# Attention heads among two weight-heavy layers: moving each reader of TensorE's results one slot behind it, and third-block scores to the front

## The chip, the cores and the metric

The kernel runs on one core of one Trainium2 chip. The metric is the device time of one execution in microseconds (us). TensorE (PE) multiplies matrices into PSUM; VectorE (DVE), ScalarE (ACT) and GpSimd (POOL) do the elementwise work; SyncE (SP) issues the DMAs. Each engine works through its own instructions in the order in which the program gives them.

## What is computed

Windowed causal attention with a linear position bias, then two dense layers with activations, all in float32:

```python
scores = scale * np.matmul(q, k.transpose(0, 1, 3, 2))     # 4 batches, 8 heads, 576 x 576, head size 64
scores = np.where(mask, scores + bias[None], -1e9)         # mask: 0 <= row - column < 128
attn = np.exp(scores - scores.max(-1, keepdims=True))
attn = attn / (attn.sum(-1, keepdims=True) + 1e-9)
x = np.matmul(attn, v)                                     # 2304 tokens x 512 (heads side by side)
h = x @ w_in                                               # 512 -> 2048
x = (h * np.clip(h + 3, 0, 6) / 6) @ w_out                 # 2048 -> 512
g = s * np.maximum(x @ w_in2, 0) ** 2 + b
out = g @ w_out2
```

## The kernel before

**Slots.** Everything up to the second layer is laid out by hand: `at(slot, rank, fn)` puts a step into a numbered slot, and the program is written slot by slot, by rank within one. Loads have rank 0 to 1, the matmuls of the first layer 10, attention matmuls 20 and more, elementwise work 30 and more. Nothing reorders it later, so an instruction that must wait holds up everything behind it on its own engine.

**The first layer** works on eight groups of tokens (four batches, first rows 0 to 255, then rows 256 to 575), each in 16 `Step`s. A step's `h` (L605) is twelve matmuls into one PSUM bank of its own tag, which all groups but the last share; `relu` (ACT, L616), `product` (DVE, L619), `hi` (ACT, L626) and `lo` (DVE, L630) turn it into two parts, and `o` (L643, twelve matmuls) of the step is four slots behind `h`. For groups 2 to 6 an odd slot holds o and h, an even slot only attention matmuls; relu and product are in the slot after h, hi and lo in the one after that. For groups 0 and 1, whose steps alternate, and for the last group h lies in the even slot.

**The heads.** Groups 0 and 1 take their heads from `StartUnit` (not changed). Those of groups 2 to 7, two at a time, are `Unit`s, planned 20 slots and more ahead of their group's first step; pairs start at slots 29, 37, 45 and so on. In what follows a place is a slot counted from a pair's first one, modulo 8. A pair goes through `load` and `load_values` (DMA), `scale` (ACT, L321), `scores` (PE, L339), `minima` (DVE, L352 and L353), `exps` (ACT, L363), `sums` (DVE, L370 and L373), `weights` (POOL, L379), `transposes` (PE, L388), `fold` (ACT, L392), `lower` (DVE, L401), `masks` (POOL, L413), `values` (PE, L428), `to_hi` (ACT, L439) and `to_lo` (DVE, L443). Groups 2 and 3 have two blocks of 128 rows a head; groups 4 to 7 have a third one of 64 rows, whose scores go into a second PSUM tile. Fold and lower read the same PSUM tile, fold first. The F tile that fold writes has one buffer.

**Places before the change.** First scores at 3, third scores at 7; minima of the even head at 3 and of the odd one at 5, of third blocks at 7 and 0; sums at 1 and 2, weights at 2 and 3; transposes, fold and lower of the even head at 4, of the odd one at 6; masks at 5 and 7; values at 1; to_hi at 2, to_lo at 3.

**PSUM.** `bank` (L148) hands out tiles. From slot 23 on three banks serve all scores, transposes and values, and the conversions of the first layer's weights. A tile asked for when none is free waits for one to be given up.

**Beside it** run the preparations of weights: `Half` (first layer, up to slot 65; L207 to L231) and `Pair` (second layer; from slot 76, every ten slots from 113 on; ACT L734, L737, L792, DVE L741, L746, L777, L796, POOL L752 and L796). Their DVE operations have ranks 37 and 38, behind those of the step and in part of the heads.

Of the kernel before, what the change touches and what calls it, by code (L numbers as in the profile page):

```python
# [23 lines left out]
def tile_alibi_window_attention_moe_moe2(  # L24
# [52 lines left out]
    def at(slot, rank, fn):  # L77
        plan.setdefault(slot, []).append((rank, len(plan[slot]), fn))
# [69 lines left out]
    def bank(name):  # L148

        nonlocal nbank  # L150
        free = 4 if slot < FIRST else 2 if slot < hslot[1, 0] else 0
        nbank += 1
        k = nbank % (3 + free)
        if k < free:
            return ps_o.tile([P, 512], F32, tag=f"o{3 - k}", name=name)
        return ps_w.tile([P, 512], F32, tag="a", bufs=3, name=name)
# [18 lines left out]
    class Half:  # L175
# [5 lines left out]
        def __init__(self, f, i, stage):  # L181
            self.f, self.i, self.stage = f, i, stage
            self.id = f"{f}_{i}"
            self.c = slice(i * DM, (i + 1) * DM)

        def plan(self, s):
            at(s - 3, 1, self.load)
            at(s, 30.1, self.high)
            at(s, 38, self.sign)
            at(s + 1, 31, self.add)  # L190
            at(s + 2, 31.2, self.hi)
            at(s + 3, 31, self.lo)

        def load(self):
            if self.stage is None:
                raw = raw_half()
            else:
                raw = wtile(self.stage, [P, 4 * DM], I32, f"stage{self.id}")[:, : 2 * DM]
            src = w1[self.f].bitcast(I32)
            nc.sync.dma_start(out=raw, in_=src[:, 2 * self.i * DM : 2 * (self.i + 1) * DM])  # L200
            raw = raw.rearrange("p (c w) -> p c w", w=2)
            self.l, self.h = raw[:, :, 0], raw[:, :, 1]
# [54 lines left out]
    class Unit:  # L257


        def __init__(self, g, b, qa, qb, h):  # L260
            self.g, self.b, self.qa, self.qb, self.h = g, b, qa, qb, h
            self.ka = max(0, qa - 1)
            self.nq = min(qb * P, S) - qa * P
            self.nk = min(qb * P, S) - self.ka * P
            self.nkb = qb - self.ka
            self.id = f"{b}_{qa}_{h}"

        def plan(self, s):
            two = min(self.qa + 2, self.qb)
            odd = self.h % 2  # L270
            s -= 4 * odd
            if not odd:
                at(s - 7, 1, self.load)
                at(s + 1, 1, self.load_values)
                at(s - 1, 34, self.scale)
                at(s + 3, 20, lambda: self.scores(self.qa, two))
                at(s + 7, 20, lambda: self.scores(two, self.qb))
            at(s + 3 + 2 * odd, 32, lambda: self.minima(self.qa, two))
            at(s + 7 + odd, 32.7, lambda: self.minima(two, self.qb))
            at(s + 5 + odd, 33, lambda: self.exps(self.qa, two))  # L280
            at(s + 8 + odd, 33, lambda: self.exps(two, self.qb))
            at(s + 9 + odd, 32.2, self.sums)
            at(s + 10 + odd, 33, self.weights)
            at(s + 12 + 2 * odd, 20, self.transposes)
            at(s + 12 + 2 * odd, 35, self.fold)
            at(s + 12 + 2 * odd, 35, self.lower)
            at(s + 13 + 2 * odd, 30.02, self.masks)
            if odd:
                at(s + 17, 20, self.values)
                at(s + 18, 39, self.to_hi)  # L290
                at(s + 19, 39, self.to_lo)

        def pair(self):
            return units[self.g * H + self.h // 2 * 2 :][:2]
# [1 line left out]
        def load(self):  # L296
            i, b = (1, self.b) if self.qa else (0, self.b - NATIVE)
            n = (self.qb - self.qa) * P
            raw = ap.tile([P, 832], F32, tag="raw", name=f"raw{self.id}")[:, : n + self.nk]
            if self.nq < n:  # L300
                nc.gpsimd.memset(raw[:, self.nq : n], 0.0)
            for u in self.pair():
                u.p = slice((u.h % 2) * D, (u.h % 2 + 1) * D)
                src = qk[i][b, u.h, u.p]
                nc.sync.dma_start(out=raw[u.p, n:], in_=src[:, self.nq :])
                nc.sync.dma_start(out=raw[u.p, : self.nq], in_=src[:, : self.nq])
                u.q = raw[:, : self.nq]
                u.X = raw[u.p, :n]
                u.rk = raw[u.p, n:]

        def load_values(self):
            i, b = (1, self.b) if self.qa else (0, self.b - NATIVE)
            rv = ap.tile([P, 2, 4 * D], F32, tag="v", bufs=2, name=f"rv{self.id}")
            rv = rv[:, :, : self.nkb * D]
            nc.sync.dma_start(out=rv, in_=vv[i][b, self.h // 2])
            for u in self.pair():
                u.rv = rv[:, u.h % 2].rearrange("p (n d) -> p n d", d=D)
# [5 lines left out]
        def square(self, i):  # L323
            o = (i - self.qa) % 2 * 256
            k0 = max(0, i - 1) * P
            k1 = min((i + 1) * P, S)
            return self.ps[(i - self.qa) // 2][:, o : o + k1 - k0], k0, k1

        def scores(self, a, b):
            for u in self.pair():  # L330
                if a == self.qa:
                    u.ps = []
                if a < b:
                    u.ps.append(bank(f"s{u.id}_{a}"))
            for i in range(a, b):
                for u in self.pair():
                    sl, k0, k1 = u.square(i)
                    q = (i - self.qa) * P
                    nc.tensor.matmul(  # L339
                        sl, lhsT=u.X[:, q : q + P], rhs=u.rk[:, k0 - self.ka * P : k1 - self.ka * P],  # L340
                        start=True, stop=True,
                    )

        def minima(self, a, b):
            if a == self.qa:
                self.Pt = ap.tile([P, 3, P], F32, tag="P", bufs=5, name=f"P{self.id}")
                self.st = ap.tile([P, 3, 3], F32, tag="st", bufs=6, name=f"st{self.id}")
            for i in range(a, b):
                sl = self.square(i)[0]
                li, r = i - self.qa, rows(i)  # L350
                if i:
                    nc.vector.copy_predicated(out=sl[:, :r], mask=own[:, :r], data=sl[:, P:])  # L352
                nc.vector.tensor_tensor_reduce(  # L353
                    out=self.Pt[:, li], in0=sl[:, :P], in1=rel if i else rel0,
                    scale=slopes[self.h], scalar=3.0e38, op0=ALU.add, op1=ALU.min,
                    accum_out=self.st[:, 0, li : li + 1],
                )
# [745 lines left out]
    for f in range(NF):  # L1103
        for i, s in enumerate((hslot[0, f], oslot[0, f])):
# [3 lines left out]
            s = min(s - 6, 3 + 4 * f + 2 * i)  # L1108
# [19 lines left out]
    for t in range(nt2):  # L1128
        u = Tokens(t)
# [118 lines left out]
```

## Time and profile before

| what | value |
|---|---|
| median of the runs shown (3) | 952.02 us (951.62 to 953.02) |
| the profiled execution | 950.19 us |
| its span, first to last instruction | 948.5 us |
| mean granted clock of TensorE in it | 0.994 |
| PE busy in the span | 904.2 us, 95% |
| DVE, ACT, POOL busy | 689.2, 508.5, 427.1 us (73, 54, 45%) |

The times in the rows below are those of the profiled execution, counted from the start of its span. A row of the timeline gives the start, the time until its last instruction ended, the engine, the line of the program, the operation, what it writes and reads, and how many instructions are merged in the row; behind it, in brackets, how long the engine had been idle and what ended that. In a row of waits stand the waiting engine and line, what it waited for, the sum in us, how many times, and the longest. Matmuls overlap, so a step's length on PE is best read from the start of its first matmul to the start of the next step's.

### The profile page before, as it was taken

To read this page: it belongs to the slowest core of one execution; us is meant where nothing else is said; L and a number is where in the kernel's file an instruction comes from. 1 tells how busy PE (TensorE), PEld (TensorE's weight loads), DVE (VectorE), ACT (ScalarE), POOL (GpSimd) and SP (SyncE) were. 2 spreads that over 40 slices of the span, in tenths; PEclk is the share of its full clock that TensorE was granted. 3 is DMA by queue.
4 is the path that set the end of the run, shared out by engine and by line. 5 is a ranking of instruction groups with operands and counts; after the bars stand their busy time and mean duration, and the time that the engine had idled before them with its cause. 6 is when DMAs were issued, how large, how long until landed. Compare 5 with 4: busy or idle time off the path is not lost.

```text
span 948.5 us, 17831 instructions
## 1 busy us (share of the span) xinstructions
PE 904.2 (95%) x6514; PEld 847.6 (89%) x6517; DVE 689.2 (73%) x1489; ACT 508.5 (54%) x1211; POOL 427.1 (45%) x563
## 2 busy tenths in 40 slices
PE   8899789899999999999999999999899997999998
PEld 4598789889898889898989999998899996999998
DVE  7999885665777766677665746779837799377792
ACT  6988665455656555555544434563415644155441
POOL 6623331323454453445442312469334497233862
PEclk9999999999999999999999999999999999999999
DMA  9443333517365446444537446874779773787763
GB/s 332 143 158 101 106 101 91 177 29 235 116 219 177 151 150 205 151 159 158 173 123 254 153 166 218 303 271 168 259 267 328 261 254 146 248 297 248 271 237 115
DMA packets 62919, 183.08 MB, mean 193 GB/s; under 512 B 7152, under 2 KB 26736, under 8 KB 54384
## 3 DMA queue, kind: packets, MB, share of 16 engines
q1 hardware_dynamic: 62832, 181.95, 56.0%
q8 instruction: 51, 0.84, 0.4%
q14 instruction: 36, 0.29, 0.1%
HBM read 143.13 MB, written 38.80 MB: 192 GB/s over the span
## 4 chain that ended last, share of the span: by engine, by line
PE 76%; DVE 15%; ACT 4%; issue 3%; DMA 1%; POOL 0%; DVEq 0%; ACTq 0%; POOLq 0%
PE h L605 19%; PE h L1045 18%; PE o L643 16%; PE o L966 15%; PE s L339 3%; DVE i L949 3%; PE v L428 3%; DVE z L212 1%; DVE x L882 1%; PE t L388 1%; DVE t L619 1%; DVE raw L746 1%; DMA wstream<-wo 1%; ACT z L207 1%; ACT F L392 1%
## 5 line engine op out<-in xcount | busy, mean ns | idle before, releaser
L605 PE MATMUL h<-x,w 128*128 128x256 f32 (+1 forms) x1536 | 230.8, 299 | 20.5 <-DVE t L619 19.9
L605 PEld LDWEIGHTS h<-x,w 128*128 128x128 f32 x1536 | 211.4, 190 | 27.6 <-DVE t L619 26.0
L643 PE MATMUL o<-g,w 128*128 128x256 f32 (+1 forms) x1536 | 235.2, 302 | 0.8 <-DVE g L630 0.6
L643 PEld LDWEIGHTS o<-g,w 128*128 128x128 f32 x1536 | 209.8, 189 | 16.5 <-issue 9.0
L966 PE MATMUL o<-wstream,i 128*128 128x256 f32 x1512 | 186.9, 286 | 13.0 <-DVE i L949 12.7
L966 PEld LDWEIGHTS o<-wstream,i 128*128 128x128 f32 x1512 | 185.2, 195 | 14.6 <-DVE i L949 14.6
L1045 PE MATMUL h<-x,wstream 128*128 128x384 f32 x1008 | 175.4, 334 | 0.0
L1045 PEld LDWEIGHTS h<-x,wstream 128*128 128x128 f32 x1008 | 174.7, 188 | 0.0
L413 POOL TENSOR_SCALAR_AFFINE_SELECT W<-F 128x128 f32<-128x128 f32 (+1 forms) x144 | 46.0, 352 | 129.6 <-ACT F L392 127.6
L619 DVE SCALAR_TENSOR_TENSOR t<-t,h 128x256 f32<-128x256 f32 (+1 forms) x128 | 57.5, 449 | 62.2 <-ACT t L616 61.7
L949 DVE TENSOR_TENSOR i<-g,i 128x768 fp32r<-128x768 f32 x60 | 95.7, 1651 | 6.2 <-issue 5.0
L616 ACT ACTIVATE t<-h 128x256 f32<-128x256 f32 (+1 forms) x128 | 52.2, 408 | 88.3 <-PE h L605 88.2
L960 POOL TENSOR_TENSOR g<-g 128x768 f32<-128x768 f32 x36 | 86.5, 2428 | 0.0
L630 DVE TENSOR_TENSOR g<-t,g 128x256 fp32r<-128x256 f32 (+1 forms) x128 | 70.6, 551 | 14.6 <-ACT g L626 13.6
L379 POOL TENSOR_SCALAR P<-P,st 128x128 f32<-128x128 f32 x128 | 54.9, 444 | 44.6 <-DVE st L373 43.9
L626 ACT ACTIVATE g<-t 128x256 fp32r<-128x256 f32 (+1 forms) x128 | 56.5, 441 | 33.8 <-DVE t L619 33.2
L1082 ACT ACTIVATE g<-g,b_sb,s_sb 128x384 f32<-128x384 f32 x96 | 62.6, 699 | 3.3 <-DVE g L1069 3.3
L401 DVE TENSOR_TENSOR W<-t,tri 128x256 f32<-128x256 f32 x48 | 20.4, 424 | 55.8 <-ACT F L392 55.5
L392 ACT ACTIVATE F<-t 128x320 f32<-128x320 f32 (+1 forms) x48 | 20.0, 417 | 70.6 <-PE t L388 70.6
L1069 DVE SCALAR_TENSOR_TENSOR g<-g 128x384 f32<-128x384 f32 x72 | 55.5, 770 | 2.5
L1090 POOL TENSOR_TENSOR i<-g,i 128x384 fp32r<-128x384 f32 x24 | 24.7, 1031 | 66.7 <-ACT i L1086 66.7
L363 ACT ACTIVATE P<-P,st 128x128 f32<-128x128 f32 x128 | 50.3, 397 | 4.0 <-DVE st L353 3.4
(119 smaller groups left out, 1213.0 us busy)
## 6 DMA issues: line engine op xcount, KB each, us to landing
wstream<-wo SPq DMA_DIRECT2D x42, 1024.0 KB, 4.9
raw<-w SPq DMA_DIRECT2D x53, 512.0 KB, 5.1
wstream<-wh SPq DMA_DIRECT2D x24, 1024.0 KB, 5.3
wstream<-wh SPq DMA_DIRECT2D x24, 768.0 KB, 4.7
wh<-staging_early SPq DMA_DIRECT2D x16, 512.0 KB, 3.2
wo<-staging_early SPq DMA_DIRECT2D x12, 512.0 KB, 3.4
stage<-w SPq DMA_DIRECT2D x11, 512.0 KB, 4.8
out<-u SPq DMA_DIRECT2D x11, 384.0 KB, 3.3
```

Source lines behind the costliest of these rows:

```text
L379: nc.gpsimd.tensor_scalar(out=pt, in0=pt, scalar1=self.st[:, 2, li : li + 1], scalar2=1.0, op0=ALU.mult, op1=ALU.mult,)
L605: nc.tensor.matmul(self.ps, lhsT=w[:, wp, cc * P : (cc + 1) * P], rhs=x[:, cc, xp], start=m == 0, stop=m == 3 * CC - 1,)
L619: nc.vector.scalar_tensor_tensor(out=self.a, in0=self.a, scalar=6.0, in1=self.ps, op0=ALU.min, op1=ALU.mult)
L626: nc.scalar.activation(self.g[:, 0], self.a, AF.Copy)
L630: nc.vector.tensor_tensor(out=self.g[:, 1], in0=self.a, in1=hi, op=ALU.subtract)
L643: nc.tensor.matmul(acc[t][d], lhsT=w[:, wp, DM + d * P : DM + (d + 1) * P], rhs=self.g[:, gp], start=f == 0 and i == 0 and (t > 1 or d % 2 ...
L949: nc.vector.tensor_tensor(out=out[:, :, 1], in0=src, in1=out[:, :, 0].bitcast(F32), op=ALU.subtract)
L960: nc.gpsimd.tensor_tensor(out=out, in0=a, in1=b, op=op)
L966: nc.tensor.matmul(self.acc[k][c], lhsT=g[:, gp, c * P : (c + 1) * P], rhs=w[:, wp * HB : (wp + 1) * HB], start=p == 0 and i == 0, stop=p ...
L1045: nc.tensor.matmul(ps, lhsT=w[:, wp, cc], rhs=x[:, cc, xp], start=start and m == 0, stop=m == 5, skip_group_check=True,)
L1069: nc.vector.scalar_tensor_tensor(out=g, in0=g, scalar=0.0, in1=g, op0=ALU.max, op1=ALU.mult)
L1082: nc.scalar.activation(g, g, AF.Identity, scale=s_sb, bias=b_sb)
```

## The change

Only `Unit` is changed. Scores of third blocks go to place 1 (rank 20.5, behind the values of an earlier pair), their minima for both heads to 2 and exponentials to 3. First scores stay at place 3, at rank 20.5. Their minima go to 4 (even) and 5 (odd), exponentials stay at 5 and 6. Sums go to 6 and 7, weights to 7 and 0 (three slots earlier within a pair). Transposes go to 3 and 5, in front of the scores of place 3. Fold and lower stay at 4 and 6 with ranks 30.3 and 32.1 in place of 35. to_hi stays at 2 with rank 30.4 in place of 39; to_lo goes to 2. `scale` stays in its slot with rank 30.5 in place of 34. Since third blocks now come first, the bookkeeping of the two score tiles and of the P tile changes with them.

```diff
+            self.Pt = None
...
-                at(s - 1, 34, self.scale)
-                at(s + 3, 20, lambda: self.scores(self.qa, two))
-                at(s + 7, 20, lambda: self.scores(two, self.qb))
-            at(s + 3 + 2 * odd, 32, lambda: self.minima(self.qa, two))
-            at(s + 7 + odd, 32.7, lambda: self.minima(two, self.qb))
+                at(s - 1, 30.5, self.scale)
+                at(s + 1, 20.5, lambda: self.scores(two, self.qb))
+                at(s + 3, 20.5, lambda: self.scores(self.qa, two))
+            at(s + 2, 32, lambda: self.minima(two, self.qb))
+            at(s + 3, 33, lambda: self.exps(two, self.qb))
+            at(s + 4 + odd, 32, lambda: self.minima(self.qa, two))
             at(s + 5 + odd, 33, lambda: self.exps(self.qa, two))
-            at(s + 8 + odd, 33, lambda: self.exps(two, self.qb))
-            at(s + 9 + odd, 32.2, self.sums)
-            at(s + 10 + odd, 33, self.weights)
-            at(s + 12 + 2 * odd, 20, self.transposes)
-            at(s + 12 + 2 * odd, 35, self.fold)
-            at(s + 12 + 2 * odd, 35, self.lower)
-            at(s + 13 + 2 * odd, 30.02, self.masks)
+            at(s + 6 + odd, 32.2, self.sums)
+            at(s + 7 + odd, 33, self.weights)
+            k = s + 2 * odd
+            at(k + 11, 20, self.transposes)
+            at(k + 12, 30.3, self.fold)
+            at(k + 12, 32.1, self.lower)
+            at(k + 13, 30.02, self.masks)
             if odd:
                 at(s + 17, 20, self.values)
-                at(s + 18, 39, self.to_hi)
-                at(s + 19, 39, self.to_lo)
+                at(s + 18, 30.4, self.to_hi)
+                at(s + 18, 39, self.to_lo)
...
-            return self.ps[(i - self.qa) // 2][:, o : o + k1 - k0], k0, k1
+            return self.ps[-1 if i < self.qa + 2 else 0][:, o : o + k1 - k0], k0, k1
...
-            if a == self.qa:
+            if self.Pt is None:
                 self.Pt = ap.tile([P, 3, P], F32, tag="P", bufs=5, name=f"P{self.id}")
```

## Rows read from the trace of the kernel before

**Rows 1.** The page's part 1: busy time, share of the span, instructions.

```profile
PE 904.2 (95%) x6514; PEld 847.6 (89%) x6517; DVE 689.2 (73%) x1489; ACT 508.5 (54%) x1211; POOL 427.1 (45%) x563
```

**Rows 2.** Waits of PE from 75 to 140 us: sum, times, longest.

```profile
PE h L605 <- DVE t L619: 8.0, 4, 2.5
PE s L339 <- DVE raw L215: 1.1, 1, 1.1
```

**Rows 3.** Waits of PE from 140 to 260 us.

```profile
PE h L605 <- DVE t L619: 5.2, 6, 2.2
```

**Rows 4.** Waits of PE from 260 to 505 us.

```profile
PE h L605 <- DVE t L619: 6.0, 11, 0.9
```

**Rows 5.** Waits of all engines from 75 to 505 us.

```profile
ACT F L392 <- PE t L388: 70.6, 40, 3.6
...
DVE W L401 <- ACT F L392: 55.5, 41, 2.4
```

**Rows 6.** Timeline of all engines around one pause of PE, 300 to 305 us.

```profile
300.03 0.48 DVE L630 TENSOR_TENSOR g<-t,g 128x320 fp32r<-128x320 f32 x1
...
301.35 0.49 PE L388 MATMUL t<-ident,P 128*128 128x128 f32 x3
...
301.59 2.00 PE L643 MATMUL o<-g,w 128*128 128x320 f32 x12
301.87 0.44 ACT L392 ACTIVATE F<-t 128x320 f32<-128x320 f32 x1 [3.15 <-PE t L388]
...
302.34 0.42 DVE L401 TENSOR_TENSOR W<-t,tri 128x256 f32<-128x256 f32 x1 [1.83 <-ACT F L392]
...
302.68 1.31 DVE L746 SCALAR_TENSOR_TENSOR raw<-raw,work 128x1024 int32<-128x1024 int32 x1
...
303.92 0.47 DVE L619 SCALAR_TENSOR_TENSOR t<-t,h 128x320 f32<-128x320 f32 x1
...
304.45 2.04 PE L605 MATMUL h<-x,w 128*128 128x320 f32 x12 [0.85 <-DVE t L619]
```

**Rows 7.** PE's part of the same timeline over the turn that follows.

```profile
306.33 0.49 PE L388 MATMUL t<-ident,P 128*128 128x128 f32 x3
...
306.75 0.60 PE L339 MATMUL s<-raw 64*128 64x192 f32 x4
...
312.37 2.02 PE L643 MATMUL o<-g,w 128*128 128x320 f32 x12
...
314.23 1.92 PE L605 MATMUL h<-x,w 128*128 128x320 f32 x12
...
316.08 1.13 PE L339 MATMUL s<-raw 64*128 64x256 f32 x8
...
319.01 1.93 PE L605 MATMUL h<-x,w 128*128 128x320 f32 x12
...
320.77 0.49 PE L388 MATMUL t<-ident,P 128*128 128x128 f32 x3
```

**Rows 8.** Timeline in one of the long pauses before 140 us, DVE.

```profile
131.04 0.42 DVE L401 TENSOR_TENSOR W<-t,tri 128x256 f32<-128x256 f32 x1 [1.42 <-ACT F L392]
```

**Rows 9.** Timelines of POOL and of DVE, 165 to 168 us.

```profile
165.42 1.89 POOL L752 TENSOR_TENSOR raw<-raw 128x1024 int32<-128x1024 int32 x1 [5.62 <-ACT y L656]
...
166.10 1.49 DVE L630 TENSOR_TENSOR g<-t,g 128x256 fp32r<-128x256 f32 x1
```

**Rows 10.** DVE's part of the timeline of rows 7.

```profile
314.30 0.49 DVE L630 TENSOR_TENSOR g<-t,g 128x320 fp32r<-128x320 f32 x1 [0.76 <-ACT g L626]
...
315.00 0.67 DVE L796 TENSOR_TENSOR raw<-work,raw 128x512 fp32r<-128x512 f32 x1
...
317.25 0.30 DVE L352 COPY_PREDICATED s<-own,s 128x128 f32<-128x128 int32 x1
...
318.46 0.49 DVE L443 TENSOR_TENSOR x<-v,x 128x320 fp32r<-128x320 f32 x1
```

**Rows 11.** Busy time of the engines and PE's granted clock, 115.4 to 118.6 us.

```profile
115.40:118.60 3.20, 3.20 (x17) 2.27 (x17) 2.65 (x8) 2.39 (x6) 0.00 (x0) 0.50 0.00 0
```

More of the change, by code (lines that the diff above doesn't have):

```diff
@@ L309, in load @@
                 u.rk = raw[u.p, n:]
+                u.ps = []
         def load_values(self):
@@ L326, in square @@
             k1 = min((i + 1) * P, S)
-            return self.ps[(i - self.qa) // 2][:, o : o + k1 - k0], k0, k1
+            return self.ps[-1 if i < self.qa + 2 else 0][:, o : o + k1 - k0], k0, k1
         def scores(self, a, b):
             for u in self.pair():
-                if a == self.qa:
-                    u.ps = []
-                if a < b:
-                    u.ps.append(bank(f"s{u.id}_{a}"))
+                u.ps.append(bank(f"s{u.id}_{a}")) if a < b else None
             for i in range(a, b):
@@ L344, in minima @@
         def minima(self, a, b):
-            if a == self.qa:
+            if self.Pt is None:
                 self.Pt = ap.tile([P, 3, P], F32, tag="P", bufs=5, name=f"P{self.id}")
```

## The prediction

> **What bounds the kernel now.** I read the busy shares first: TensorE (PE) is busy 95% of the span [rows 1], more than VectorE (DVE), ScalarE (ACT) or GpSimd (POOL). So time is won only where PE stands still or does work that can go. Next I read who keeps PE waiting in the stretch where the later heads run, 75 to 505 us. Nearly all of it is one wait: the h-matmuls of a step (L605) wait for the product of the step before (DVE, L619), because all h-sums of groups 0 to 6 share one PSUM bank. It is 8.0 us in 4 waits up to 140 us, 5.2 us in 6 up to 260 us, and 6.0 us in 11 after that [rows 2 to 4]. The reader should see 21 pauses, not a steady loss.
>
> Then I read what DVE itself waits for: 55.5 us, 41 times, `lower` (L401) waits for `fold` (ACT, L392), which reads the same bank before it; and fold waits 70.6 us, 40 times, for the transposes [rows 5]. One pause shows how the two hang together [rows 6]. PE does h, then the transposes at 301.35, then o at 301.59. Fold and lower stand in the slot of the transposes, so ACT sits idle 3.15 us until PE has made them, and DVE idles 1.83 us before lower at 302.34. Queued behind lower are a long operation of the weight preparation (L746, 1.31 us) and the product, which starts at 303.92. PE, done with o, waits for it until 304.45. DVE was not short of time; it waited and then had to do everything at once. From o's first matmul to the next h 2.86 us pass here, against 1.86 where nothing waits (312.37 to 314.23) [rows 6, 7]: the pause costs 1.00 us and is recorded as 0.85 idle, so I add 0.15 us to every recorded wait.
>
> **The change part by part.** I count places 0 to 7 in the eight-slot turn of a pair, its first slot being 0; for the middle groups o and h come at even places.
>
> Fold, lower and transposes: transposes go to places 3 and 5, fold and lower stay at 4 and 6, ahead of the Pair operations. PE now runs a whole o and h between the transposes and the product that follows, so neither fold nor lower waits for PE. After 260 us the waits are 6.0 + 11 x 0.15 = 7.6 us [rows 4], and DVE's 1.83 us of idleness in the typical pause exceeds its 1.00 us of loss [rows 6]. I take all 7.6; bounds 3 and 7.6, since minima is added to place 4. Between 140 and 260 us they are 5.2 + 6 x 0.15 = 6.1 [rows 3]; the longest (2.2) lies where Pair 0 crowds several operations into one slot and stays in part, so I take 4.0; bounds 2 and 6.1.
>
> Up to 140 us the weights of the first layer are still being prepared (Half). There fold waits for no transpose: it stands behind exponentials and conversions on ACT, DVE idles 1.42 us in front of lower at 131.04 [rows 8], and the product comes later still. The ACT burst is not moved; fold only passes the exponentials of its slot. Of 8.0 + 4 x 0.15 = 8.6 us [rows 2] I take 1.0 as gained; bounds 0 and 8.6.
>
> Scores: third-block scores move from place 7 (behind the odd transposes) to 1 (behind the values), and the even transposes from o-and-h's place 4 to 3, ahead of the other scores. PE's runs of attention work in a turn go from four (values; scores; transposes; transposes with third scores) to three. A run costs PE at its edges: o after one takes 1.86, h before scores 1.85 (314.23 to 316.08), against 1.76 before a transpose (319.01 to 320.77) [rows 7]: 0.09 and 0.10. Changing from transposes to scores inside a run takes 0.42 (306.33 to 306.75) where transposes to o take 0.24 (301.35 to 301.59) [rows 6, 7], so 0.18. Before, a turn pays 2 x 0.19 for values and for scores, some 0.08 and 0.28 for the transposes; after, 0.19, 0.28 and 0.08, plus 0 to 0.2 for changing from values to scores, which no row shows. The saving is 0 to 0.19 in 16 turns (groups 4 to 7, four pairs each): 1.5, bounds 0 and 3. The eight turns of groups 2 and 3 have no third block and I put them at nothing.
>
> Minima, exponentials, sums, weights: the instructions are the same in number. Two full blocks of minima take 1.21 us of DVE (317.25 to 318.46) [rows 10], and the two narrower third blocks at place 2 no more. Even minima go from place 3 to 4, in front of lower, and odd ones stay at 5. Sums go from places 1 and 2 to 6 and 7, so that one head's stand in front of the product behind place 6: two operations on three columns, between nothing and one block of minima (0.6); I take 0.4. All of it lies under PE's 3.6 us of o and h unless a Pair operation of 1.3 us or more falls into places 5 and 6; that happens about once in five turns, and I charge 0 to 0.8 us each time, 1.0 in all.
>
> To_lo and the banks: `to_lo` (L443) goes from the end of place 3 to the end of place 2, because place 3 now takes all three free banks (even transposes, two scores). The last score must wait until to_lo has given up the values' bank. What is queued in front of to_lo on DVE? By the old trace, lo at 314.30, then the thirds' minima (up to 1.2, new), then L796 at 0.67 (315.00, now later), then to_lo at 0.49: done near 317.0. The last score would start near 317.15 (316.08, half a microsecond later for the third scores moved ahead, 0.57 for transposes and first score) [rows 7, 10]. That just fits; with L746 in L796's place (1.31) it is 0.5 late. I charge 2.0 us over the run; bounds 0 and the rival below.
>
> The rest: `scale` and `to_hi` only pass other ACT work in their slots; their pair's load is still issued eight slots before the first score, so at SP's queue I see no price. Fold has one F tile, which the masks on POOL read in the next slot: the odd fold, two slots on, waits only if POOL is over 3 us behind. Weights leave places 2 and 3 for 7 and 0, three slots or more ahead of the transposes. If those covers were gone, a late fold would hold relu and then the product as now. I put them at nothing; the bounds above hold them.
>
> **Sum:** 7.6 + 4.0 + 1.0 + 1.5 - 1.0 - 2.0 = 11.1 us. The profiled execution took 950.19 us (span 948.5), 1.83 below the median of the runs, 952.02. Against the profile it gives 939.1, against the median 940.9.
>
> **A rule that speaks against it.** At 166.10 lo (L630), 0.48 us at 300.03 [rows 9, 6], took 1.49 us, while POOL's L752 ran from 165.42 for 1.89 us: DVE's subtraction ended shortly after POOL was through [rows 9]. The Trainium skill ("SBUF — State Buffer", SBUF: two separate sides) says that DVE operations with two SBUF inputs and GpSimd operations share a port pair as an exclusive lock, and the loser waits for the whole instruction. The trace agrees. By that rule the moved POOL work decides anew which subtractions lose, and the sum comes out as in rival 1, or unchanged if no more of them lose than now.
>
> **Rivals.**
> 1. *POOL takes the gain back.* Weights and masks now meet other DVE subtractions; one collision costs 1.0 us [rows 9, 6]. For: lo, the Pair subtractions and POOL's long operations share the same slots. Against: POOL is busy only 45% [rows 1]. With half a microsecond uncovered in half of the 24 turns, 6 us go back: 947.
> 2. *The banks stop PE: slower.* Place 3 needs three banks, and to_lo is last in DVE's slot. For: the trace has one such wait, scores for L215, 1.1 us [rows 2]; to_lo now runs 2.4 us after the scores begin (316.08 to 318.46) [rows 7, 10]. Against: product and minima, which are in front of it now, then stand behind it. At 1.1 us in each of 24 turns it costs 26 us against a gain without it of 14.1 - 1.0 = 13.1 (the 1.0 being the crowding): 965. The point of balance is 13.1/24 = 0.55 us a turn.
> 3. *The early stage is freed too.* If fold's earlier rank and the lighter places 1 and 2 take away most of the 8.6 us [rows 2] too, and with them the stretch from 115.4 to 118.6 us in which the granted clock was 0.50, that is 1.2 GHz, just behind such a pause [rows 11], another 6 to 9 us go: 934. Against: ACT is full there [rows 8].
> 4. *It does nothing:* the product is as late by minima and sums in front of it as it was by lower. Then 952. Against: DVE's idle time in rows 5.
>
> **How the numbers follow.** My forecast (8 to 15 us gained) gets 0.57, rival 1 (2 to 8 gained) 0.17, rival 3 0.12, rival 4 0.05, rival 2 0.09. The likeliest gives 941. The range takes in the bounds of the forecast's costs, all of rival 1 and most of rival 3, down to 932 and up to 949; rivals 2 and 4 and the rest of 3 are left out. Measurements of this kernel can tell about 0.2%, 1.9 us. Faster by more: 0.57 + 0.17 + 0.12 = 0.86; same 0.05; slower 0.09.
>
> **What would show it.** Right: L401 and L392 no longer wait (55.5 us near zero), L605's wait for L619 after 140 us falls from 11.2 to under 4, PE shows values and third scores as one run. Wrong: scores or transposes waiting for L443 by several microseconds (rival 2), L619 still late behind L353, L373 or a stretched L630 (rivals 1 and 4). A wait for PE at fold or lower of its old size would make the whole prediction wrong.

## The result and the profile after

The changed kernel takes 943.49 us in the median of five runs (941.91 to 947.97), against 952.24 us (951.62 to 953.02) for the kernel before in the same runs: a ratio of 0.9917, 95% interval 0.9888 to 0.9947. That is 8.75 us less by the medians. The profiled execution took 942.24 us; its span is 940.5 us against 948.5, so 8.0 us less.

The page's part 1, kernel after:

```profile
PE 901.5 (96%) x6514; PEld 848.0 (90%) x6517; DVE 692.2 (74%) x1489; ACT 505.0 (54%) x1211; POOL 437.1 (46%) x563
```

As in [rows 1], PE is the only engine near its limit, and every engine has as many instructions as before. By stretches, as in [rows 2 to 4], the waits of PE are (after; 75 to 140, 140 to 260 and 260 to 505 us in this order):

```profile
PE h L605 <- DVE t L619: 8.1, 4, 2.1
PE s L339 <- DVE stage L215: 0.7, 1, 0.7
...
PE h L605 <- DVE t L619: 2.2, 2, 1.4
...
PE s L339 <- DVE x L443: 1.2, 2, 0.8
PE o L643 <- DVE g L630: 0.8, 1, 0.8
PE h L605 <- DVE t L619: 0.4, 2, 0.2
```

Up to 140 us nothing moved (8.0 to 8.1). After that L605's wait for L619 fell from 11.2 us in 17 waits to 2.6 in 4, and new waits appeared: scores for `to_lo` (L443) and o for `lo` (L630). The waits of all engines from 75 to 505 us, as in [rows 5]:

```profile
DVE t L619 <- ACT t L616: 69.5, 66, 2.6
DVE g L630 <- ACT g L626: 23.5, 41, 1.7
...
DVE W L401 <- ACT F L392: 3.2, 6, 0.7
```

`lower` waiting for `fold` is down from 55.5 us, 41 times, to 3.2 us, 6 times; fold's wait for the transposes (70.6 us) has left the list. The two long waits of DVE that remain are those of the steps themselves: the product waits for `relu` (69.5 us), `lo` for `hi` (23.5 us).

**Reading the gain by steps.** Both kernels run the same h and o on PE in the same order (only attention matmuls move among them), so the start of a step in one timeline less its start in the other is the lead won so far. I take three marks: the 27th h on PE (141.20 us before), the 58th (261.81) and the first matmul of the second layer, L1045 (569.34 before, 561.37 after). The last two columns are the lead won between the first mark and the third, and how many stretches of 3.4 us at a granted clock of 0.50 (1.2 GHz) the profile has between 75 and 145 us. The kernels of the experiments stand in the same table:

```
lead over before, us   27th h   58th h   layer 2   end of span   won 27th h to layer 2   at 1.2 GHz, 75-145
before                   0.0      0.0      0.0        0.0               0.0                  1
after                    1.69     4.39     7.97       8.0               6.28                 0
after_again             -1.16     1.55     5.15       3.7               6.31                 2
readers_alone           -2.82     0.49     6.66       6.7               9.48                 2
sums_behind              0.36     4.75     9.64       6.7               9.28                 3
sums_again               0.66     5.07     9.97       8.7               9.31                 2
tolo_ahead              -1.53     1.19     5.97       4.5               7.50                 2
sign_behind              0.67     3.42     7.01       5.5               6.34                 0
all_behind               2.38     4.88     9.39       6.4               7.01                 0
early_pool              -3.84     0.55     5.47       5.4               9.31                 3
before_sign             -5.09    -5.08    -4.99      -5.0               0.10                 2
minima_at_4             -1.74    -2.64    -2.56      -2.5              -0.82                 2
fold_back               -3.17    -7.22   -13.66     -16.6             -10.49                 3
fold_back_sums          -1.42    -3.28    -8.78     -10.3              -7.36                 1
```

The reader should see two things. Between the first and the third mark the clock is full in these profiles (fold_back and minima_at_4 have one stretch each there), and the two executions of the changed program agree to 0.03 us (6.28 and 6.31): this is what the change does. At the first mark they differ by 2.85 us, with no slow stretch in the one and two in the other. Two rows of busy time by window, after first, then its repetition (columns: time, then busy us and instructions of PE, PEld, DVE, ACT, POOL, granted clock, DMA share, GB/s):

```profile
75.00:140.00 65.00, 55.60 (x442) 50.81 (x441) 58.20 (x144) 47.49 (x122) 28.67 (x38) 1.00 0.35 109
```

```profile
75.00:140.00 65.00, 56.38 (x425) 51.36 (x423) 57.43 (x137) 46.28 (x120) 28.32 (x37) 0.95 0.36 108
```

The kernel before had 0.97 in this window, with the one stretch of [rows 11]. So the 1.69 us by which after leads at the 27th h are no shorter waits (8.0 and 8.1 us). At 75 us the lead was 0.27; it fell to -2.00 at the 15th h and was back at -0.12 at the 21st; then 1.49 us came between the 21st and the 22nd h, where only the kernel before has a stretch at half the clock.

**Where the lead after 140 us comes from.** The lengths of three pieces in ten successive turns (from about 294 us on), each from its first matmul to the next piece's first: o at place 6, o at place 0, and the two blocks of scores at place 3.

```
before          o at 6: 2.85 1.84 2.32 1.84 2.52 2.86 1.84 2.32 1.84 2.52
                o at 0: 1.90 2.23 1.86 1.86 1.86 1.90 2.23 1.86 1.86 1.86
                scores: 1.06 in all ten
after           o at 6: 1.84 1.84 1.84 1.84 1.83 1.84 1.84 1.84 1.84 1.84
                o at 0: 1.76 2.17 1.76 1.76 2.42 1.76 1.88 1.76 1.76 2.42
                scores: 1.37 1.06 1.06 1.06 2.50 1.06 1.06 1.06 2.16 1.06
```

All the old pauses are gone, at both places. New ones stand at place 0 and in the scores, fewer but not smaller. The 2.17 in the second turn at place 0 is one of them, not the old 2.23: lower waits for nothing there, but lower, the sums and a Pair operation (L746) are queued in front of the product. Where nothing waits, o at place 0 takes 1.76 in place of 1.86, since no attention matmuls stand before it any more.

### The profile page after: what moved, and what is told of

The parts are those of the page before. It is cut to its first block, busy times and chain, and to the rows that moved or that the text cites. A ratio compares the mean times of both kernels' runs of the same rounds, so it can differ in the third digit from the quotient of the medians.

```text
span 940.5 us, 17984 instructions
## 1 busy us (share of the span) xinstructions
PE 901.5 (96%) x6514; PEld 848.0 (90%) x6517; DVE 692.2 (74%) x1489; ACT 505.0 (54%) x1211; POOL 437.1 (46%) x563
## 4 chain that ended last, share of the span: by engine, by line
PE 75%; DVE 15%; ACT 3%; issue 3%; DMA 2%; SPq 0%; DVEq 0%; ACTq 0%
PE h L1045 19%; PE h L605 17%; PE o L643 17%; PE o L966 15%; PE s L339 3%; DVE i L949 3%; PE v L428 3%; DVE x L882 1%; DVE z L212 1%; DVE g L630 1%; PE t L388 1%; DVE work L777 1%; DMA wstream<-wo 1%; DVE t L619 1%; ACT z L207 1%
## 5 line engine op out<-in xcount | busy, mean ns | idle before, releaser
L605 PE MATMUL h<-x,w 128*128 128x256 f32 (+1 forms) x1536 | 228.3, 298 | 11.9 <-DVE t L619 11.1
L605 PEld LDWEIGHTS h<-x,w 128*128 128x128 f32 x1536 | 212.1, 190 | 15.3 <-DVE t L619 14.6
L1045 PE MATMUL h<-x,wstream 128*128 128x384 f32 x1008 | 175.4, 334 | 0.0
L1045 PEld LDWEIGHTS h<-x,wstream 128*128 128x128 f32 x1008 | 174.7, 188 | 0.0
L619 DVE SCALAR_TENSOR_TENSOR t<-t,h 128x256 f32<-128x256 f32 (+1 forms) x128 | 57.6, 450 | 86.4 <-ACT t L616 86.3
L413 POOL TENSOR_SCALAR_AFFINE_SELECT W<-F 128x128 f32<-128x128 f32 (+1 forms) x144 | 45.4, 347 | 125.5 <-ACT F L392 125.5
L630 DVE TENSOR_TENSOR g<-t,g 128x256 fp32r<-128x256 f32 (+1 forms) x128 | 70.3, 549 | 29.7 <-ACT g L626 29.0
L379 POOL TENSOR_SCALAR P<-P,st 128x128 f32<-128x128 f32 x128 | 67.6, 544 | 9.8 <-DVE st L373 7.6
L1069 DVE SCALAR_TENSOR_TENSOR g<-g 128x384 f32<-128x384 f32 x72 | 55.5, 770 | 2.5
L1078 POOL TENSOR_TENSOR g<-g 128x384 f32<-128x384 f32 x24 | 22.7, 945 | 60.8 <-ACT g L1074 60.8
L1074 ACT ACTIVATE g<-h 128x384 f32<-128x384 f32 x24 | 11.8, 492 | 69.4 <-PE h L1045 69.4
```

What stands on the lines that cost most here:

```text
L379: nc.gpsimd.tensor_scalar(out=pt, in0=pt, scalar1=self.st[:, 2, li : li + 1], scalar2=1.0, op0=ALU.mult, op1=ALU.mult,)
L605: nc.tensor.matmul(self.ps, lhsT=w[:, wp, cc * P : (cc + 1) * P], rhs=x[:, cc, xp], start=m == 0, stop=m == 3 * CC - 1,)
L619: nc.vector.scalar_tensor_tensor(out=self.a, in0=self.a, scalar=6.0, in1=self.ps, op0=ALU.min, op1=ALU.mult)
L630: nc.vector.tensor_tensor(out=self.g[:, 1], in0=self.a, in1=hi, op=ALU.subtract)
L1045: nc.tensor.matmul(ps, lhsT=w[:, wp, cc], rhs=x[:, cc, xp], start=start and m == 0, stop=m == 5, skip_group_check=True,)
L1069: nc.vector.scalar_tensor_tensor(out=g, in0=g, scalar=0.0, in1=g, op0=ALU.max, op1=ALU.mult)
```

## The experiments

### The readers alone, and the readers put back

readers_alone is the kernel before with only the readers of PE moved:

```diff
-            at(s + 12 + 2 * odd, 20, self.transposes)
-            at(s + 12 + 2 * odd, 35, self.fold)
-            at(s + 12 + 2 * odd, 35, self.lower)
+            at(s + 11 + 2 * odd, 20, self.transposes)
+            at(s + 12 + 2 * odd, 30.3, self.fold)
+            at(s + 12 + 2 * odd, 32.1, self.lower)
...
-                at(s + 18, 39, self.to_hi)
-                at(s + 19, 39, self.to_lo)
+                at(s + 18, 30.4, self.to_hi)
+                at(s + 18, 39, self.to_lo)
```

> The kernel before, with only transposes a slot earlier, fold and lower at ranks 30.3 and 32.1, and to_hi and to_lo as in the change (a bank must be free at place 3); scores, minima, sums and weights stay where they were. Theory (the gain comes from fold and lower no longer waiting for PE): L605's wait for L619 after 140 us falls from 11.2 us to under 4, and the time is 6 to 9 us under the kernel before. Rival (the gain comes from scores, minima and the three runs of attention work): the waits stay at 8 or more and the time is within 2 us of before.

Measured: 944.24 us, ratio 0.9912 (0.9899 to 0.9925). The gain of the whole change, from its smaller half (to_hi and to_lo moved with the other readers and were not tried without them). Waits of PE in readers_alone, 140 to 260 and 260 to 505 us:

```profile
PE t L388 <- POOL P L379: 1.8, 2, 1.2
PE h L605 <- DVE t L619: 1.5, 2, 1.0
...
PE s L339 <- issue: 0.5, 1, 0.5
```

After 260 us L619 no longer appears. Transposes a slot earlier now sometimes wait for the weights (L379), which the full change avoids by moving sums and weights forward. By steps readers_alone wins 9.48 us after 140 us, more than the full change (6.28): the rest of the change costs 3.2 us there.

fold_back is the kernel after with those three steps back in place:

```diff
-            at(k + 11, 20, self.transposes)
-            at(k + 12, 30.3, self.fold)
-            at(k + 12, 32.1, self.lower)
+            at(k + 12, 20, self.transposes)
+            at(k + 12, 35, self.fold)
+            at(k + 12, 35, self.lower)
```

> The changed kernel with transposes, fold and lower put back into one slot (rank 20 and 35, places 4 and 6), all else as changed. Theory: L401 waits for L392 some 50 us again, L605's wait for L619 after 140 us is back at 9 us or more, the time within 3 us of the kernel before. Rival: waits under 5 us, the time within 2 us of the changed kernel.

Measured: 965.85 us, ratio 1.0130 (1.0110 to 1.0149), 14 us slower than before. Waits of all engines and of PE alone from 260 to 505 us, fold_back:

```profile
ACT F L392 <- PE t L388: 62.4, 39, 3.5
DVE W L401 <- ACT F L392: 41.4, 41, 2.3
...
PE h L605 <- DVE t L619: 10.8, 19, 0.9
```

The old waits of DVE and ACT are back [rows 5], and with them the old pause, as the theory said. But there are 19 of them after 260 us in place of 11 [rows 4], and the time is far above that of before. So something in the rest of the change makes the old arrangement worse. Two suspects: the sums in front of the product, and the place of the scores.

### What made the old arrangement worse

fold_back_sums puts the sums and weights of fold_back where they were before; minima_at_4 moves only the first minima in the kernel before.

```diff
-            at(s + 6 + odd, 32.2, self.sums)
-            at(s + 7 + odd, 33, self.weights)
+            at(s + 9 + odd, 32.2, self.sums)
+            at(s + 10 + odd, 33, self.weights)
```

> The run fold_back with sums and weights where they were in the kernel before (places 1 and 2, 2 and 3). Theory (sums in front of the product, stretched while POOL works, make fold_back slower than the kernel before): the time falls from 966 to 956 or less. Rival (the even minima, in front of lower at place 4, or the other order of scores do it): it stays above 961.

Measured: 961.51 us, ratio 1.0105 (1.0088 to 1.0121), so the sums make up some 4 us of the 14.

```diff
-            at(s + 3 + 2 * odd, 32, lambda: self.minima(self.qa, two))
+            at(s + 4 + odd, 32, lambda: self.minima(self.qa, two))
```

> The kernel before with the even head's minima at place 4, in front of lower, and no longer at 3. Theory (fold_back_sums is 9 us slower than the kernel before since the third scores no longer stand between the odd transposes and the next o and h, and so no longer give the late product 0.7 us of cover a turn): minima change nothing, within 1.5 us of the kernel before. Rival (minima in front of lower make the product late): 5 us or more slower.

Measured: 953.57 us, ratio 1.0010 (1.0000 to 1.0020), with PE's waits for L619 at 8.5, 4.9 and 6.1 us. Minima in front of lower cost nothing. The third scores are left, and the lengths show them at work, in the same ten turns as above:

```
fold_back_sums  o at 6: 2.85 1.84 2.32 1.84 2.52 2.85 1.84 2.32 1.83 2.52
                o at 0: 2.60 2.93 1.84 2.40 2.00 2.60 2.93 1.84 2.40 2.00
```

Place 6 is as before to 0.01 us. At place 0 the same turns are up to 0.70 us longer (1.90 to 2.60, 2.23 to 2.93). Of the 8.78 us lost by the second layer, 5.5 are lost after the 58th h: place 0 costs some 6.5 us more there than before and scores that come late 1.3, and the run of attention work that falls away gives a part back. One such pause in fold_back (timeline):

```profile
334.57 0.49 PE L388 MATMUL t<-ident,P 128*128 128x128 f32 x3
...
334.81 2.00 PE L643 MATMUL o<-g,w 128*128 128x320 f32 x12
...
337.21 0.48 DVE L619 SCALAR_TENSOR_TENSOR t<-t,h 128x320 f32<-128x320 f32 x1
...
337.75 1.45 PE L605 MATMUL h<-x,w 128*128 128x320 f32 x8 [0.93 <-DVE t L619]
```

and the same step in the kernel before:

```profile
324.62 0.49 PE L388 MATMUL t<-ident,P 128*128 128x128 f32 x3
...
325.04 0.60 PE L339 MATMUL s<-raw 64*128 64x192 f32 x4
...
325.56 2.03 PE L643 MATMUL o<-g,w 128*128 128x320 f32 x12
...
327.27 0.47 DVE L619 SCALAR_TENSOR_TENSOR t<-t,h 128x320 f32<-128x320 f32 x1
...
327.80 1.44 PE L605 MATMUL h<-x,w 128*128 128x320 f32 x8 [0.21 <-DVE t L619]
```

From the transposes to the product's end both take the same time (3.12 us), and so does the pause's end. Before, PE had the third scores to do in that time (0.53 us, and 0.18 more for changing to them); in fold_back it had nothing and stood 0.93 us instead of 0.21. Third scores were cover for the odd half of the old wait. They could only be moved away because the readers were moved a slot behind.

### The sums in front of the product

In the kernel after, the longest pause left after 140 us lies at 204 us. Timeline of the kernel after:

```profile
202.22 2.00 POOL L752 TENSOR_TENSOR raw<-raw 128x1024 int32<-128x1024 int32 x1 [3.68 <-DVE raw L746]
202.38 0.42 DVE L401 TENSOR_TENSOR W<-t,tri 128x256 f32<-128x256 f32 x1
202.72 1.53 DVE L370 TENSOR_SCALAR st<-st 128x3 f32<-128x3 f32 x1
...
204.37 0.39 DVE L619 SCALAR_TENSOR_TENSOR t<-t,h 128x256 f32<-128x256 f32 x1
204.82 1.46 PE L605 MATMUL h<-x,w 128*128 128x256 f32 x10 [1.43 <-DVE t L619]
```

The addition on 128 x 3 numbers (L370), 0.15 us at its shortest, takes 1.53 us and ends with POOL's L752; the product stands behind it. sums_behind puts both heads' sums behind the product of place 7:

```diff
-            at(s + 6 + odd, 32.2, self.sums)
+            at(s + 7, 32.2, self.sums)
```

> The changed kernel with the even head's sums at place 7, behind the product, and no longer at 6 in front of it. Theory (the sums, stretched to 1.53 us while POOL's L752 runs, made the product late at 204 us): the waits of L605 for L619 after 140 us fall from 2.6 us to 1.2 or less, the time falls by 1 to 2 us against the changed kernel. Rival (the product is late for the operations of the weight preparation, whatever the sums do): waits within 0.5 us of 2.6 and no change of the time over 0.5 us.

Measured: 941.31 us, ratio 0.9879 (0.9860 to 0.9897). By steps it wins 9.28 us after 140 us, 3.0 more than after. Because the interval of after was wide, both programs were run again, unchanged, on one chip:

> The changed kernel itself, on the chip of the three runs beside it, as their measure. Both theories expect 943 us within 2.

> The run sums_behind once more, beside the changed kernel on one chip. Theory (the sums in front of the product cost 2 us): 1.5 to 3 us under the changed kernel. Rival (the difference was one of chips and of where stretches at 1.2 GHz fell): within 1 us.

Measured: 944.87 us for after_again, ratio 0.9921 (0.9907 to 0.9935), and 940.23 us for sums_again, ratio 0.9874 (0.9861 to 0.9887): 4.6 us apart, more than expected. By steps 9.31 against 6.31, so 3.0 belong to the edit after 140 us in both pairs; of the remainder up to 140 us I can say only that the wait for L619 there was 6.9 against 7.9 us. Waits of PE in sums_again after 260 us:

```profile
PE s L339 <- DVE x L443: 1.5, 3, 0.8
```

L619 has left PE's list. Four additions are still held beside POOL's L752 (1.20 to 1.85 us), but now the weights wait for sums (24.1 us in 22 waits of POOL from 75 to 505 us) and not the product. This is the best version found, 11 to 12 us below the kernel before.

### The banks

tolo_ahead moves `to_lo` in front of the Pair operations of its slot:

```diff
-                at(s + 18, 39, self.to_lo)
+                at(s + 18, 36, self.to_lo)
```

> The changed kernel with to_lo at rank 36 of its slot, in front of the preparation of weights, no longer at 39 behind it. Theory (the scores at place 3 wait for the bank that to_lo gives up late): the waits of L339 for L443, 1.2 us after 260 us and some before, go to 0, and 1 to 2 us are gained. Rival (the bank is not what the scores wait for, or a later step takes the place): the time stays within 0.5 us.

Measured: 942.47 us, ratio 0.9892 (0.9877 to 0.9907), not to be told from after. Waits of PE after 260 us:

```profile
PE t L388 <- DVE st L353: 1.5, 2, 1.0
```

L443 is gone, and transposes wait for the minima (L353) instead, which now come later: going by recorded waits, nothing won. The steps say otherwise: 7.50 us against 6.28, so 1.2 are won. The scores that took 2.50 and 2.16 us take 1.37 each, 1.9 less, and the h behind them, which the late transposes end, takes 0.2 and 0.7 more. sums_behind with this edit was not run.

### The early stage

Here PE's waits did not change. In the long pauses up to 140 us the preparation of the first layer's weights (L212, L215) stands in front of the product (timeline of the kernel after):

```profile
95.75 0.68 DVE L212 TENSOR_SCALAR z<-z 128x512 int32<-128x512 int32 x1
96.46 0.69 DVE L215 SCALAR_TENSOR_TENSOR stage<-stage,z 128x512 int32<-128x512 int32 x1
97.07 0.41 DVE L619 SCALAR_TENSOR_TENSOR t<-t,h 128x256 f32<-128x256 f32 x1
97.53 0.74 PE L605 MATMUL h<-x,w 128*128 128x256 f32 x4 [2.06 <-DVE t L619]
```

sign_behind moves those (L212 to L215, one `Half` in each turn) behind the product of the next slot; all_behind adds later exponentials and sums; before_sign is the kernel before with the first edit alone. Their later lines are one higher.

```diff
-            at(s, 38, self.sign)
-            at(s + 1, 31, self.add)
+            late = s % 8 == 3 and s > 30
+            at(s + late, 31.6 if late else 38, self.sign)
+            at(s + 1, 32 if late else 31, self.add)
```

> The changed kernel with one step of Half (sign, DVE L212 and L215, and POOL's add behind it) put behind the product of the next slot, in those four slots (35, 43, 51, 59) in which a pair's place 6 meets it. Theory (the four pauses up to 140 us, 8.1 us, last as long as DVE works on sign in front of the product; relu is done 1.0 us earlier): each pause falls by about 1.0 us, L605's wait for L619 up to 140 us from 8.1 to about 4, and 3 to 5 us are gained. Rival (ACT is full there, and the product would be late in any case, as the prediction put it): the waits stay above 7 and the time changes by less than 1 us.

> The kernel before with that one step of Half moved in the same four slots, and nothing else. Theory (the early pauses have nothing to do with the change, and are DVE's order in both kernels): L605's wait for L619 up to 140 us falls from 8.0 to 4 or less, and 3 to 5 us are gained. Rival (before the change lower itself, late behind fold, held the product): waits of 6 or more, less than 2 us gained.

```diff
-            at(s + 5 + odd, 33, lambda: self.exps(self.qa, two))
-            at(s + 6 + odd, 32.2, self.sums)
+            at(s + 5 + 2 * odd, 33, lambda: self.exps(self.qa, two))
+            at(s + 7 + odd, 32.2, self.sums)
```

> The changed kernel with sign as in the run before, and besides the odd head's exponentials at place 7 behind relu (they stood at 6, in front of the next relu on ACT), and sums at 7 and 0 behind the products. Theory (product and relu each wait for work that could come behind them): L605's wait for L619 from 75 to 505 us falls from 10.7 to 3 or less, and the time to 933 to 937 us. Rival (a later step takes the place: weights come late on POOL, transposes wait for them, or the scores wait for banks): those waits grow by 2 us or more and the time stays above 938.

Measured: sign_behind 945.62 us, ratio 0.9932 (0.9918 to 0.9946); before_sign 955.33, 1.0047 (1.0030 to 1.0063); all_behind 942.64, 0.9909 (0.9895 to 0.9923). None wins over its starting point with certainty, and the kernel before loses. Waits of PE up to 140 us in sign_behind:

```profile
PE h L606 <- DVE t L620: 5.2, 8, 1.1
PE s L340 <- DVE raw L216: 2.2, 2, 1.1
PE o L644 <- DVE g L631: 0.7, 1, 0.7
PE s L340 <- DVE stage L216: 0.7, 1, 0.7
```

Four pauses became eight shorter ones, and the moved operation now holds up the scores (L340): 8.8 us in all, where the kernel after had 9.4. At the 27th h sign_behind leads by 0.67 us and after by 1.69, neither with a slow stretch. In before_sign the wait for L216 is 4.5 us. all_behind, which has the shortest waits for the product (3.7 us), leads by 2.38 us there, but after 140 us it wins only 7.01 us, 2.3 less than sums_behind; its recorded waits of scores and transposes there are longer (4.3 us against 2.4 in sums_again), and which of its moves does that was not separated.

early_pool is sums_behind with the subtraction of the first layer's weights on POOL:

```diff
+            self.pool = s > 30
...
-            nc.vector.tensor_tensor(
+            (nc.gpsimd if self.pool else nc.vector).tensor_tensor(
```

> sums_behind with one more operation of Half (lo, L231, 0.7 to 1.5 us of DVE a time) given to POOL from slot 31 on. Theory (the pauses up to 140 us are DVE's whole load there, 58 of 65 us, so moving work about within DVE gives nothing and taking work away does): DVE busy from 75 to 140 us falls by 10 us or more, L605's wait for L619 there from 6.4 to 3 or less, and the time by 3 to 5 us. Rival (POOL, which is busy 29 of 65 us there, makes DVE's other operations longer while it works, or is late itself): the waits stay above 5 and less than 1 us is gained.

Measured: 943.18 us, ratio 0.9905 (0.9892 to 0.9918), 3 us above sums_again. Busy time from 75 to 140 us, and the steps' `lo` (L631 here, L630 elsewhere) in the same window, in early_pool:

```profile
75.00:140.00 65.00, 55.30 (x403) 50.11 (x403) 50.02 (x122) 46.13 (x119) 41.56 (x51) 0.92 0.33 104
```

```profile
L631 DVE TENSOR_TENSOR g<-t,g 128x256 fp32r<-128x256 f32 x15 | 12.3, 822 | 2.0 <-ACT g L627 1.7 <-ACT w L228 0.3
```

DVE has 5.6 us less to do than in sums_again (55.65), although the operations moved had taken 11.8 us there: each `lo` of a step now takes 822 ns where it took 441. The lead at the 27th h is 4.2 us lower than in sums_behind, with three slow stretches in each, and the lead won after that is the same 9.3. So neither another order on DVE nor this work's move to POOL frees the early stage. A DVE with 10 us less to do, as the theory asked, was not reached, and ACT's burst was not moved; what would free the stage is open.

## Why the prediction was right, point by point

**Forecast and range.** 941 (932 to 949) was predicted, 943.49 measured, faster as forecast. The mechanism is the one argued: the wait of lower for fold is gone, the product is in time, and readers_alone shows that this part makes the gain; fold_back, which takes back transposes, fold and lower but not to_hi and to_lo, has the old pauses again. But the net after 140 us was predicted as 7.6 + 4.0 + 1.5 - 1.0 - 2.0 = 10.1 us and came to 6.3 by steps. Gains and costs were both too small, the costs by more (3.0 predicted, 11.7 measured). That 941 came within 2.5 us of the median is in part luck: the two errors have opposite signs, and of the 8.0 us between the two profiles 1.5 come from the stretch at half the clock that only the kernel before had.

**Pauses removed: 7.6 and 4.0 predicted, all of both measured.** After the 58th h the eleven old pauses were 7.8 us by their lengths over an undisturbed o, and none is left at either place; between the marks at 141 and 262 us none of the six is left either, 6.2 us by their lengths, where 4.0 were taken. What remains in the records there (2.2 us) are new pauses elsewhere.

**Fewer runs: 1.5 predicted, 3.0 by the lengths.** The unknown was what the change from values to scores costs. Timeline of the kernel after:

```profile
306.18 1.31 PE L428 MATMUL v<-W,rv 128*64 128x128 f32 x16
307.42 0.60 PE L339 MATMUL s<-raw 64*128 64x192 f32 x4
307.94 2.03 PE L643 MATMUL o<-g,w 128*128 128x320 f32 x12
```

Values take 1.24 us (306.18 to 307.42), as they took in front of o before, and third scores 0.52. The change costs nothing, so the upper bound, 0.19 in each of 16 turns, is what is saved.

**Crowding: 1.0 charged, about 5.8 measured.** The place was right: o at place 0 waits for a product that stands behind lower, one head's sums and Pair operations. The lengths there exceed 1.76 (1.44 in the turns with 256 columns) by 1.43, 0.41, 0.66, 0.12 and 0.66 after 262 us, 3.3 in all, and by 1.59 and 0.88 in two turns before it. The mis-sized term is "about once in five turns, and I charge 0 to 0.8 us each time": it was seven turns after 140 us alone, at 0.8 us on average and up to 1.6. Of the 5.8 us 2.5 are left with the sums out of the way (sums_again), where lo and lower stand behind Pair operations (L777 and L796, 2.6 us together, at 283 and 376 us). In front of a product only one addition was held by POOL, the 1.53 us at 202.72, and its turn lost 1.59; in the other six the two operations took 0.3 to 0.4 us, as the prediction had it ("I take 0.4"), and cost 0.1 to 0.4 each. The prediction applied POOL's lock to subtractions alone, which have two SBUF inputs. The Trainium skill ("SBUF — State Buffer", Who interferes with whom) also counts a `tensor_scalar` with one input, where it runs in a two-port mode. The trace agrees that such an operation loses (1.53 us); whether the mode is the reason no run here shows.

**Banks: 2.0 charged, about 5.9 measured.** This was rival 2's mechanism at a quarter of its price. The prediction's case is "with L746 in L796's place it is 0.5 late". With L746 alone nothing is late; the lines up to the first dots are such a turn, those behind them the worst one (timelines, after):

```profile
273.95 1.22 DVE L746 SCALAR_TENSOR_TENSOR raw<-raw,work 128x1024 int32<-128x1024 int32 x1
275.08 0.48 DVE L443 TENSOR_TENSOR x<-v,x 128x320 fp32r<-128x320 f32 x1
275.87 1.13 PE L339 MATMUL s<-raw 64*128 64x256 f32 x8
...
364.36 0.89 DVE L657 TENSOR_SCALAR y<-o 128x320 f32<-128x320 f32 x2 [1.81 <-PE o L643]
365.37 0.49 DVE L630 TENSOR_TENSOR g<-t,g 128x320 fp32r<-128x320 f32 x1
...
366.73 1.22 DVE L746 SCALAR_TENSOR_TENSOR raw<-raw,work 128x1024 int32<-128x1024 int32 x1
367.87 0.48 DVE L443 TENSOR_TENSOR x<-v,x 128x320 fp32r<-128x320 f32 x1
368.40 1.13 PE L339 MATMUL s<-raw 64*128 64x256 f32 x6 [0.78 <-DVE x L443]
```

At 367 us the record says 0.78 us, the length of these scores 2.50 against 1.06, so 1.44 lost. The prediction's list of what is queued in front of to_lo lacks L657, with which DVE copies the finished sums of a group's o. It waits for PE itself (1.81 us idle), and lo, the minima and to_lo stand behind it: lo starts 0.92 us after the first matmul of its h (364.45), where the prediction had 0.07 (314.30 and 314.23) [rows 7, 10]. This list is the step of the prediction that failed. Of the six scores that came late between the first and the third mark, five have L657 in front of lo: alone it cost 0.3 us (227 and 294 us), with a Pair operation behind it 1.44 and 1.10. In the fifth (165 us) and in the one without it (259 us) lo itself took 1.19 and 1.59 us beside POOL's L752. No run moved L657, so its share stays a reading of the traces. After the 58th h four late scores lost 0.82, 0.31, 1.44 and 1.10, in sum 3.7, and transposes that came late 1.0; before that 1.2 more. tolo_ahead, which took to_lo from behind the Pair operations, got back 0.78, 1.13 and 0.79 of the first, third and fourth.

Rivals 1 and 4 were therefore partly true: rival 4 by sums and Pair operations in front of the product, rival 1 by one held addition and two stretched lo.

The terms again: 7.8 + 6.2 + 3.0 - 5.8 - 5.9 = 5.3. The h behind a late product is 0.1 us longer too, 1.8 us in all before and 0.8 after, which gives 6.3; measured 6.3.

**Early stage: 1.0 predicted, nothing measured.** The waits stayed at 8.1 us. Rival 3 asked for the slow stretch of [rows 11] to go with them. In the profile of after it was gone, in its repetition two were there, so it is no effect of the change.

**Nothing for scale, to_hi, masks, minima:** nothing here speaks against it; scale and to_hi were not tried alone. Minima were tried alone (0 to 0.2% longer); POOL's masks wait for fold as before (125.5 us against 127.6), and nobody on the path waits for them.

**The signs named:** L401's and L392's waits near zero, yes; L619 after 140 us under 4 us, yes (2.6); values and third scores as one run, yes; no scores waiting for several us on L443, by the records (1.2) yes, by the lengths barely.

## What to carry to other kernels

With engines that keep their order, put a step that reads TensorE's results a slot behind the matmuls: DVE stood idle in front of lower and then had to do lower, a long operation and the product in one go. Look for every such reader: the one that was not moved (L657) stood in front of five of the six late scores. Before moving work off a wait, see what it covers: the third scores hid 0.7 us of each odd pause, and with them moved away but not the readers the kernel was 1% slower. And size pauses by the start of one step to the start of the next, against an undisturbed turn; the recorded waits gave a third of what the banks cost.

## What the runs showed of the hardware that was not expected

An operation of DVE on 128 x 3 numbers with one SBUF tensor took 1.53 us beside POOL's L752 and 0.15 us without it. A long POOL operation held up even the smallest DVE operation of this kind. The kernel before shows it too, so it could have been read before the forecast:

```profile
349.42 1.89 POOL L752 TENSOR_TENSOR work<-raw 128x1024 int32<-128x1024 int32 x1 [3.46 <-ACT t L616]
349.55 1.80 DVE L370 TENSOR_SCALAR st<-st 128x3 f32<-128x3 f32 x1
```

Changing from values to scores inside a run costs PE nothing, from transposes to scores 0.18 us (0.42 against 0.24).

The stretches at 1.2 GHz come at different steps in executions of the same program (two between 75 and 145 us in after_again, none in after), and what one costs depends on where it falls. Windows of the second layer, one each of before, after and sums_behind, which are the same program there:

```profile
658.00:661.40 3.40, 3.39 (x16) 3.39 (x17) 3.40 (x2) 1.49 (x3) 3.40 (x2) 0.51 0.00 0
650.00:653.40 3.40, 3.36 (x16) 3.36 (x16) 3.40 (x2) 1.51 (x3) 3.40 (x2) 0.50 0.00 0
664.40:667.80 3.40, 3.40 (x19) 3.40 (x18) 3.40 (x7) 2.31 (x4) 0.00 (x0) 0.50 1.01 427
```

In before and after the stretch falls at the same step, 8.0 us apart, and the lead of 7.97 us at the start of the second layer is 8.0 at its end. In sums_behind it falls at a later step, where PE is busy all of the 4 us behind it; the lead of 9.64 shrinks by 1.5 us there, by 1.5 more at a second stretch, and is 6.7 at the end. So single executions of these kernels differ by more than some of the edits do (941.91 to 947.97 for after), while the lead won between two marks at full clock agrees to 0.03 us.
